# Splitting the operands of the last two FFN groups: which engine does which step, when the second weights are split, and where the pieces are kept

## The chip, the cores and the metric

The kernel runs on one core of one Trainium2 chip. The metric is device time in microseconds (us), the median of several executions. One more execution of each kernel is taken with the hardware profiler; its own time and its span are given beside the median. The core has five engines with a queue each: TensorE (PE, matrix products; its weight loads are shown as PEld), VectorE (DVE), ScalarE (ACT), GpSimd (POOL) and SyncE (SP, which issues most DMAs). Each engine takes its instructions in the order in which the program was built; an instruction that waits holds up everything behind it on its engine.

## The reference

Eight sequences of 576 tokens with eight heads of 64 go through an attention whose scores are cut off below the row's maximum less tau; the result, 4608 tokens of 512 numbers, goes through a feed-forward layer (FFN) with an ELU. Everything is float32.

```python
scores = scale * np.matmul(q, k.transpose(0, 1, 3, 2))
thresh = np.max(scores, axis=-1, keepdims=True) - tau
scores = np.where(scores >= thresh, scores, -1000000000.0)
attn = np.exp(scores - np.max(scores, axis=-1, keepdims=True))
attn = attn / (np.sum(attn, axis=-1, keepdims=True) + 1e-09)
x = np.matmul(attn, v)                       # bridged to (4608, 512)
h = x @ w_in                                 # w_in  512 x 2048
g = np.where(h > 0.0, h, np.exp(np.minimum(h, 0.0)) - 1.0)
out = g @ w_out                              # w_out 2048 x 512
```

## The kernel before, in words

**Groups.** The FFN works on nine groups of 512 tokens: eight hold the first 512 tokens of each sequence, and the ninth collects the 64 last tokens of all eight (`xtail`). Group 0 is done plainly, groups 1 to 6 by one level of Strassen's scheme in fp32 (lines 1675 and 1815), mixed with the attention of later sequences. For Strassen some blocks of the weights in SBUF have been replaced by differences (`change_in`, `change_out`); `restore_in` (L2055) and `restore_out` (L2059) add them back. The last Strassen group also needs sums of blocks of its hidden values, `sums` (L1762), which go through a queue of small jobs, `extra`, of which one is taken now and then (`run_extra`). While attention is still running (`attending`), these sums are GpSimd's. The adds at L1824 to L1835 take Strassen products out of the PSUM banks; the next product in the bank waits for them.

**The last two groups**, g7 and g8 (B - 1 and B), are done in split precision. An operand X is cut into a rounded part a = X(1 - 2^-13) held as fp32r, on ScalarE (`cut`, L1997; for weights L2021), and a rest b = X - a (`rest`, L2001; for weights L2026), and a cross piece is made from both (`cross`, L2005; for weights L2032). Three fp32r matmuls on these pieces stand in for one fp32 matmul. For weights the rest is also scaled by 2^12 (`weights_scaled`, L2029). The split of a token part costs an ACT step, a two-operand step on VectorE or GpSimd (an argument says which), and a VectorE step. The split of a weight tile costs an ACT step, a two-operand step on GpSimd, an ACT step, and a VectorE step.

**First product.** For each of 16 rows f of 128 hidden units and each of the two groups, `first_round` (L2182) runs eight matmuls into one of eight PSUM banks, ACT scales the bank (L2186), and `cross_round` (L2195) adds four more. Then come the exponential (ACT, L2206), minus one (GpSimd, L2209) and the ELU (VectorE, L2212). The five first rows of g7 go ahead, so that the parts of g8 have time to be made. **Second product.** `second` (L2261) runs three matmuls for each row and each of four token blocks; all of g7, then all of g8, with the first three and the last three rows taken block by block (`EDGE`). The cross weights of g8 are made afresh (L2252). At the end of a group each block's two banks are put together by ACT (L2276) and VectorE (L2278) and stored.

**Order.** This tail is written with a clock of its own: `at(t, f)` puts an instruction on an agenda at an estimated time, and `on_pe` records everything due before each piece of TensorE's work. The times fix the order in every queue, and nothing else; the hardware's waits do the rest. `UNIT` and `ONE` are the estimated times of twelve matmuls and of one.

**Places.** The pieces live in 24 slots on the right of SBUF (`r0` to `r23`) and 34 on the left (`l0` to `l33`), taken from the front of `free` and given back at its end. Names in the profile are those of the slots. The rounded part of eight second-weight rows goes into the upper half of the first weights, dead by then (`w_in_hi`); raw hidden values of the later rows go into the lower half (`w_in_lo`) and into token tiles (`xt`).

Of the kernel before, what the change touches and what calls it, by code (L numbers as in the profile page):

```python
# [368 lines left out]
def kernel(  # L369
# [10 lines left out]
    nc = tc.nc  # L380
# [61 lines left out]
    HF = DF // 2  # L442
    w_in_sb = [const.tile([P, KJ, HF], FP32, name=x) for x in ("w_in_lo", "w_in_hi")]

    def w_in_at(j, f, n):
        return w_in_sb[f // HF][:, j, f % HF : f % HF + n]

    w_out_sb = const.tile([P, NFT, DM], FP32, name="w_out_sb")
# [13 lines left out]
    pieces += [(moe_w_out, w_out_sb[:, f, n : n + WN], f, n) for f in range(NFT) for n in range(0, DM, WN)]  # L462
# [683 lines left out]
    def ffn2_plain(c, i, part):  # L1146
        def run(k):
# [3 lines left out]
            nc.tensor.matmul(cur[c, i][:, :DM], hidden(c, ft % NU, 1)[:, 0, ft // NU, i], w_out_sb[:, ft],  # L1151
# [101 lines left out]
    def make_out(r):  # L1253
        rooms = []

        def one(k, p):
# [3 lines left out]
            b12, b11 = w_out_sb[:, u : u + 2, HM:], w_out_sb[:, u : u + 2, :HM]  # L1260
            b21, b22 = w_out_sb[:, NU + u : NU + u + 2, :HM], w_out_sb[:, NU + u : NU + u + 2, HM:]
# [10 lines left out]
    def change_out(u):  # L1272
        b12, b11 = w_out_sb[:, u : u + 2, HM:], w_out_sb[:, u : u + 2, :HM]
        extra.append((1.3, "out", lambda: nc.gpsimd.tensor_tensor(b12, b12, b11, ALU.subtract)))
# [337 lines left out]
    with tc.manual_schedule():  # L1612
# [172 lines left out]
        def second_round(g, r):  # L1785
            banks_ = []

            def chunk(c):
# [5 lines left out]
                def quarter(m, k):  # L1794
# [15 lines left out]
                    for v in range(2 * k, 2 * k + 2):  # L1810
# [3 lines left out]
                               w_out_sb[:, right[1] * NU + u, right[2] * HM : (right[2] + 1) * HM])  # L1814
# [153 lines left out]
        free, parts, split_stack = deque(), {}, ExitStack()  # L1968
# [5 lines left out]
        def slot(dt):  # L1974
            pool, name = home = free.popleft()
            return pool.tile([P, DM], dt, name=name), home

        def drop(key, *which):
            for x in which or range(len(parts[key])):
                if parts[key][x] is not None:  # L1980
                    if parts[key][x][1]:
                        free.append(parts[key][x][1])
                    parts[key][x] = None
# [15 lines left out]
        def rest(key, src, engine, cols=slice(0, DM), fresh=True):  # L1999
            b = take(key, F32R) if fresh else parts[key][1][0]  # L2000
            engine.tensor_tensor(b[:, cols], src()[:, cols], parts[key][0][0].bitcast(FP32)[:, cols], ALU.subtract)  # L2001
# [6 lines left out]
        def split_tokens(t, key, src, engine):  # L2008
            at(t, lambda: cut(key, src))
            at(t + 0.8, lambda: rest(key, src, engine))  # L2010
            at(t + (0.8 if engine is nc.gpsimd else 1.5), lambda: cross(key, src))

        def weights_cut(key, src):
            if key[0] == "out" and EDGE <= key[1] < EDGE + NU:
# [312 lines left out]
```

## Time and profile before

| | us |
|---|---|
| median of 3 runs (lowest to highest) | 1275.36 (1274.95 to 1275.61) |
| profiled execution, its own time | 1273.53 |
| its span in the profile | 1271.7 |
| end of the last wide attention step's products (L1815 follows) | 1048.2 |
| first split matmul (L2182) | 1082.3 |
| first matmul of the second product (L2261) | 1173.5 |
| last matmul ends | 1267.0 |

Busy time in four stretches of the tail, in us: Strassen's end, the first product, the second product of g7 with its edges, the second product of g8.

| stretch | PE | DVE | ACT | POOL |
|---|---|---|---|---|
| 1050 to 1077 | 23.77 | 15.42 | 5.88 | 16.48 |
| 1100 to 1165 | 65.00 | 25.18 | 38.07 | 35.09 |
| 1165 to 1215 | 46.82 | 49.93 | 31.55 | 30.36 |
| 1215 to 1272 | 52.04 | 37.33 | 12.09 | 15.47 |

A timeline line gives start, duration, engine, line of the program, operation, tiles written and read, shapes and count; in brackets the engine's idle time before it and what ended that. Matmuls overlap, so the pace is read from starts, not from durations. On VectorE, ScalarE and GpSimd an instruction's record also holds time in which it stood but could not go on.

### The profile page before, as it was taken

What the parts mean: (1) busy time and instruction counts of PE and PEld (TensorE: products, weight loads), DVE (VectorE), ACT (ScalarE), POOL (GpSimd) and SP (SyncE); (2) the same over time, 40 slices, a digit from 0 to 9 for tenths busy, and PEclk for the clock granted to TensorE, in tenths of its full rate; (3) what the DMA queues carried; (4) which work ended last, traced back from release to release, by engine and by line L of the source; (5) the groups of instructions that cost most, each with busy time, mean ns of one, the idle gap of its engine ahead of it and who ended that gap; (6) DMA issues with size and microseconds to landing.
All of it is one profiled execution on the core that took longest, in us unless ns stands there. A gap on an engine that the chain in (4) does not pass through costs nothing.

```text
span 1271.7 us, 21210 instructions
## 1 busy us (share of the span) xinstructions
PE 1246.8 (98%) x6598; PEld 957.3 (75%) x6598; DVE 1035.4 (81%) x2146; ACT 651.2 (51%) x1363; POOL 804.6 (63%) x1114
## 2 busy tenths in 40 slices
PE   8999999999999999999999999999999998999998
PEld 5675576467778787878887787878787886788876
DVE  7888777788898979898889888997989885635994
ACT  7899776664443525262535344443525261556630
POOL 4778665677585748585676657674768475466650
PEclk9999999999999999999999999999999999999999
DMA  7466688998889998999889898989899864000001
GB/s 142 147 174 186 170 244 233 258 269 208 229 228 258 239 252 231 250 247 229 236 238 276 217 234 215 252 241 233 231 265 249 228 198 149 3 1 1 1 34 34
DMA packets 325553, 245.75 MB, mean 193 GB/s; under 512 B 209216, under 2 KB 289984, under 8 KB 325440
## 3 DMA queue, kind: packets, MB, share of 16 engines
q1 hardware_dynamic: 323264, 243.65, 71.6%
q8 instruction: 52, 0.85, 0.3%
q10 hardware_dynamic: 2176, 0.75, 0.2%
q14 instruction: 61, 0.50, 0.1%
HBM read 154.53 MB, written 89.78 MB: 192 GB/s over the span
## 4 chain that ended last, share of the span: by engine, by line
PE 87%; DVE 5%; issue 2%; DMA 2%; ACT 2%; POOL 1%; SPq 1%; ACTq 0%; DVEq 0%; POOLq 0%
PE f L1815 22%; PE f L1675 22%; PE sc L974 8%; PE sc L1047 7%; PE f L2182 4%; PE f L1099 4%; PE f L2261 4%; PE sc L670 3%; PE f L1151 3%; PE pv L927 2%; PE f L2195 2%; PE rt L789 1%; PE sc L1039 1%; PE sc L1034 1%; DMA there<-x 1%
## 5 line engine op out<-in xcount | busy, mean ns | idle before, releaser
L981 DVE TENSOR_REDUCE mx<-sc 128x1 f32<-128x576 f32 x207 | 148.3, 750 | 29.2 <-PE sc L974 25.2
L723 POOL TENSOR_SCALAR w<-w,rs 128x576 f32<-128x576 f32 x144 | 116.3, 816 | 70.4 <-DVE rs L786 69.7
L1001 ACT ACTIVATE w<-sc,mx 128x576 f32<-128x576 f32 x113 | 81.5, 739 | 115.1 <-DVE mx L981 98.1
L865 DVE STREAM_TRANSPOSE x<-w 128x512 f32<-128x512 f32 (+1 forms) x153 | 108.9, 744 | 14.0 <-POOL w L723 11.3
L993 POOL TENSOR_SCALAR th<-mx,ntau 128x2 f32<-128x2 f32 (+1 forms) x114 | 34.1, 299 | 132.8 <-DVE mx L981 132.8
L974 PE MATMUL sc<-kT,qT 64*128 64x448 f32 (+4 forms) x736 | 102.8, 416 | 0.0
L974 PEld LDWEIGHTS sc<-kT,qT 64*128 64x128 f32 x736 | 81.0, 186 | 24.3 <-issue 16.2
L1008 DVE SCALAR_TENSOR_TENSOR w<-sc,th,w 128x576 f32<-128x576 f32 x113 | 88.2, 810 | 9.5 <-ACT w L1001 9.2
L1815 PE MATMUL f<-t,s 128*128 128x256 f32 x384 | 91.7, 380 | 3.2 <-POOL s L1762 3.1
L1675 PE MATMUL f<-xt,sw 128*128 128x256 f32 x384 | 93.6, 386 | 0.7 <-ACT g L1737 0.5
L1815 PE MATMUL f<-w_out_sb,g 128*128 128x256 f32 x384 | 92.0, 382 | 0.0
L1815 PE MATMUL f<-w_out_sb,s 128*128 128x256 f32 x384 | 91.9, 382 | 0.0
L723 POOL TENSOR_SCALAR e<-e,rs 128x576 f32<-128x576 f32 x91 | 67.3, 744 | 35.2 <-DVE rs L786 33.8
L1815 PEld LDWEIGHTS f<-t,s 128*128 128x128 f32 x384 | 72.5, 190 | 14.9 <-POOL s L1762 5.2
L1675 PEld LDWEIGHTS f<-xt,sw 128*128 128x128 f32 x384 | 69.3, 189 | 17.3 <-issue 5.0
L1815 PEld LDWEIGHTS f<-w_out_sb,g 128*128 128x128 f32 x384 | 72.0, 190 | 12.5 <-issue 3.2
L1815 PEld LDWEIGHTS f<-w_out_sb,s 128*128 128x128 f32 x384 | 71.9, 190 | 12.1 <-issue 2.5
L1762 POOL TENSOR_TENSOR s<-g 128x256 f32<-128x256 f32 x96 | 75.9, 795 | 7.3 <-DVE g L1725 6.8
L1001 ACT ACTIVATE e<-sc,mx 128x576 f32<-128x576 f32 x91 | 66.5, 744 | 24.6 <-DVE mx L981 23.2
L1008 DVE SCALAR_TENSOR_TENSOR e<-sc,th,e 128x576 f32<-128x576 f32 x91 | 71.2, 810 | 7.6 <-ACT e L1001 7.6
L865 DVE STREAM_TRANSPOSE x<-e 128x640 f32<-128x640 f32 x92 | 66.0, 755 | 1.0
L727 DVE TENSOR_REDUCE mx<-sc 128x1 f32<-128x576 f32 x81 | 59.3, 747 | 5.5 <-PE sc L670 5.1
(323 smaller groups left out, 3283.7 us busy)
## 6 DMA issues: line engine op xcount, KB each, us to landing
there<-x SPq DMA_DIRECT2D x444, 144.0 KB, 3.6
wTb<-there SPq DMA_DIRECT2D x58, 576.0 KB, 6.3
wTa<-there SPq DMA_DIRECT2D x53, 576.0 KB, 5.1
sw<-win_sums SPq DMA_DIRECT2D x46, 384.0 KB, 4.8
t<-wout_sums SPq DMA_DIRECT2D x33, 512.0 KB, 6.3
qm<-in_q_dram SPq DMA_DIRECT2D x124, 72.0 KB, 4.9
wst<-in_moe_w_in_dram SPq DMA_DIRECT2D x16, 512.0 KB, 4.2
vm<-in_v_dram SPq DMA_DIRECT2D x64, 128.0 KB, 3.6
```

What stands on the lines that cost most here:

```text
L723: nc.gpsimd.tensor_scalar(wv, wv, st["rs"][:, h : h + 1], 1.0, ALU.mult, ALU.mult)
L727: nc.vector.tensor_reduce(st["mx"][:, h : h + 1], st[h][:, :, :HALF], axis=AX.XY, op=ALU.max, negate=True)
L865: nc.vector.transpose(x[:, :, c0 : c0 + nc_], src.rearrange("p (c g n) -> p g c n", c=nc_, n=T))
L974: on_banks(nc.tensor.matmul(o, qT[r, i * P : (i + 1) * P], kT[r, k0 : k0 + n], start=True, stop=True, skip_group_check=True), o)
L981: on_banks(nc.vector.tensor_reduce(st["mx"][:, h : h + 1], st["sc", h], axis=AX.XY if i == NC else AX.X, op=ALU.max, negate=True), st["sc" ...
L1001: on_banks(nc.scalar.activation(st["e", h], st["sc", h], AF.Exp, bias=st["mx"][:, h : h + 1]), st["sc", h])
L1008: on_banks(nc.vector.scalar_tensor_tensor(st["e", h], st["sc", h], st["th"][:, h : h + 1], st["e", h], ALU.is_ge, ALU.mult, accum_out=st[" ...
L1047: on_banks(nc.tensor.matmul(o, vm[:, h, c], parts[part][:, g0:g1, h * (NC + 1) + c], start=False, stop=(c == NC - 1), skip_group_check=Tru ...
L1099: nc.tensor.matmul(loc["ph"][:, k], w_in_at(j, ft * P, P), xts[g][:, j, hf * CT : (hf + 1) * CT], start=(j == 0), stop=(j == KJ - 1))
L1675: nc.tensor.matmul(loc["banks"][place], left[:, j], right[:, j], start=(begins and j == 0), stop=(j == 1), skip_group_check=True)
L1762: engine.tensor_tensor(o, x, y, op)
L1815: nc.tensor.matmul(place(m), lhs, rhs, start=(begins and v == 0), stop=(v == RU - 1), skip_group_check=True)
```

## The change

- Every two-operand step of the splits is VectorE's: the rests of tokens and of weights, and `restore_out`. The weights' rest becomes scaled on GpSimd (a one-operand step) instead of ACT, and the weights' cross piece is a plain subtraction on VectorE, made for second weights once for each group (`cross, g, f`) and no longer at their split.
- Eleven of the sixteen second-weight rows are split beside the first product, from 22 us after its start, one every 3.9 us; `restore_out` begins at 16 us, every 3.6 us.
- The weights lie in four tiles each (`w_in0` to `w_in3`, `w_out0` to `w_out3`) instead of two halves and one tile. When the last row of a quarter is split, `give` hands the quarter on as four slots for pieces of one type, which are taken ahead of the others. The token tiles are handed on likewise. The tiles kept for raw hidden values go.
- Before the first product three weight tiles are split instead of two, all eight lower restores are done there, and of g8 only one token part. Splitting begins one us earlier on the agenda.
- When splitting begins, `attending` is set to False, which gives the Strassen sums but the third to VectorE; in the last pair's step the jobs of `extra` are put on the agenda 1.9 us apart.
- Four rows of g7 go ahead, not five; the estimated times are raised.
- For the last token block the matmuls of the last three rows run first for the first bank (and the rest pieces), then for the cross pieces, and ACT's scaling is recorded between them.

```diff
-    w_in_sb = [const.tile([P, KJ, HF], FP32, name=x) for x in ("w_in_lo", "w_in_hi")]
+    w_in_sb = [const.tile([P, KJ, QF], FP32, name=f"w_in{x}") for x in range(4)]
+    w_out_sb = [const.tile([P, NFT // 4, DM], FP32, name=f"w_out{x}") for x in range(4)]
...
+        def give(pool, name, dt):
+            t = pool.tile([P, KJ, DM], dt, name=name)
+            kept_for[dt].extend(t[:, x] for x in range(KJ))
+
-        def slot(dt):
+        def slot(dt, wide=True):
+            if kept_for[dt]:
+                t = kept_for[dt].popleft()
+                return t, lambda: kept_for[dt].append(t)
             pool, name = home = free.popleft()
...
-        def rest(key, src, engine, cols=slice(0, DM), fresh=True):
+        def rest(key, src, cols=slice(0, DM), fresh=True):
             b = take(key, F32R) if fresh else parts[key][1][0]
-            engine.tensor_tensor(b[:, cols], src()[:, cols], parts[key][0][0].bitcast(FP32)[:, cols], ALU.subtract)
+            nc.vector.tensor_tensor(b[:, cols], src()[:, cols], parts[key][0][0].bitcast(FP32)[:, cols], ALU.subtract)
...
-            engine.tensor_tensor(like(d[0], src()), src(), like(parts[key][0][0].bitcast(FP32), src()), ALU.subtract)
+            d = take(("d", key), FP32)
+            nc.vector.tensor_tensor(like(d, src()), src(), like(parts[key][0][0].bitcast(FP32), src()), ALU.subtract)
 
         def weights_scaled(key):
-            nc.scalar.activation(take(key, F32R), parts["d", key][0][0], AF.Copy, scale=1.0 / EPS)
+            nc.gpsimd.tensor_scalar(take(key, F32R), parts["d", key][0][0], 1.0 / EPS, None, ALU.mult)
 
         def weights_cross(key):
-            nc.vector.scalar_tensor_tensor(take(key, F32R), parts["d", key][0][0], 1.0 / EPS,
-                                           parts[key][0][0].bitcast(FP32), ALU.mult, ALU.subtract)
-            drop(("d", key))
+            c, d = (parts[key][x][0].bitcast(FP32) for x in range(2))
+            nc.vector.tensor_tensor(take(key, F32R), d, c, ALU.subtract)
...
-        def split_weights(t, key, src, engine):
+        def split_weights(t, key, src, then=None):
             at(t, lambda: weights_cut(key, src))
-            at(t + 0.7, lambda: weights_rest(key, src, engine))
-            end = t + (2.3 if engine is nc.gpsimd else 1.6)
-            at(end, lambda: weights_scaled(key))
-            at(end + 0.1, lambda: weights_cross(key))
+            at(t + 0.7, lambda: (weights_rest(key, src), then and then()))
+            at(t + 1.4, lambda: (weights_scaled(key), drop(("d", key))))
+            if key[0] == "in":
+                at(t + 2.1, lambda: weights_cross(key))
...
-            nc.gpsimd.tensor_tensor(b12, b12, b11, ALU.add)
+            nc.vector.tensor_tensor(b12, b12, b11, ALU.add)
...
+        EARLY_IN = 3
 
         def split_begin():
             t = now[0]
+            attending[0] = False
...
+            for f in range(EARLY_IN):
+                at(t + 0.2 + 3.2 * f, lambda f=f: restore_in(f))
+                split_weights(t + 0.6 + 3.2 * f, ("in", f), w_in_of(f))
             for j in range(KJ - 1):
-                split_tokens(t + 0.2 + 2.2 * j, ("x", B - 1, j), x_of(B - 1, j), nc.vector)
-            for f in range(2):
-                at(t + 6.6 + 3.0 * f, lambda f=f: restore_in(f))
-                split_weights(t + 7.2 + 3.0 * f, ("in", f), w_in_of(f), nc.gpsimd)
-            for j in range(2):
-                split_tokens(t + 13.0 + 2.4 * j, ("x", B, j), x_of(B, j), nc.vector)
+                split_tokens(t + 2.2 + 3.2 * j, ("x", B - 1, j), x_of(B - 1, j))
+            split_tokens(t + 12.0, ("x", B, 0), x_of(B, 0))
+            for f in range(NU, NFT):
+                at(t + 11.0 + 1.2 * (f - NU), lambda f=f: restore_in(f))
...
-                at(t + 13.0, split_begin)
+                at(t + 12.0, split_begin)
+                for x in range(8):
+                    at(t + 1.0 + 1.9 * x, lambda: run_extra(max(0.9, extra[0][0])) if extra else None)
...
-        UNIT, ONE = 2.58, 0.215
+        UNIT, ONE, LEAD, AHEAD = 2.73, 0.2272, 8.0, 4
...
+        for j, t in ((1, 0.9), (2, 4.6), (last, 7.4)):
+            split_tokens(begin + t, ("x", g8, j), x_of(g8, j),
+                         (lambda: [give(xpool, "xt", FP32) for _ in range(2)]) if j == last else None)
...
+        for f in range(EARLY_IN, NFT):
+            t = max(begin + 0.4 + 3.4 * (f - EARLY_IN), start_of[g7, f] - LEAD)
+            if f < NU:
+                at(t - 0.5, lambda f=f: restore_in(f))
+            split_weights(t, ("in", f), w_in_of(f), lambda f=f: in_done(f))
         for u in range(NU):
-            at(begin + 30.0 + 5.0 * u, lambda u=u: restore_out(u))
+            at(begin + 16.0 + 3.6 * u, lambda u=u: restore_out(u))
...
+        OUT_EARLY = 11
         for f in range(NFT):
...
+            split_weights(begin + 22.0 + 3.9 * f if f < OUT_EARLY else start_f(middle, f) - 9.0, ("out", f), w_out_of(f),
+                          lambda f=f: out_done(f))
+            for g, t0 in ((g7, middle), (g8, end)):
+                t = start_f(t0, f) - (9.5 if f < EDGE else 6.0) + 2.9 * f * (f < EDGE)
+                split_tokens(t, ("h", g, f), g_of(g, f), lambda g=g, f=f: drop(("g", g, f)))
+                at(t + 2.2, lambda g=g, f=f: nc.vector.tensor_tensor(
+                    take(("cross", g, f), F32R), parts["out", f][1][0].bitcast(FP32), parts["out", f][0][0].bitcast(FP32),
+                    ALU.subtract))
...
+        def edge(g, fs, i):
+            if (g, i) == (g8, 3) and fs[-1] == NFT - 1:
+                return [(lambda f=f, xs=xs: second(g, f, i, xs), len(xs) * ONE) for xs in ((0, 1), (2,)) for f in fs]
+            return [(lambda f=f: second(g, f, i), 3 * ONE) for f in fs]
```

146 lines of the change are left out of this document (59 added, 87 removed).

## The prediction

> **What bounds the kernel now.** I read the page's busy shares first, then the chain of work that ended last, then the waits of the last 240 us, then the timelines of TensorE (PE), VectorE (DVE) and GpSimd (POOL) there, because the order in which the changed program is built agrees with the old one on every engine up to about 1050 us. Only the last two of nine FFN groups differ, and the sums that end the group before them.
>
> ```profile
> PE 1246.8 (98%) x6598; PEld 957.3 (75%) x6598; DVE 1035.4 (81%) x2146; ACT 651.2 (51%) x1363; POOL 804.6 (63%) x1114
> ```
>
> TensorE is the bound, so a gain can only come from time in which it does not stream. The waits name who keeps it (total, times, longest):
>
> ```profile
> PE f L2261 <- DVE r L2032: 3.2, 2, 2.5
> PE f L1815 <- POOL s L1762: 3.1, 2, 2.9
> PE f L2182 <- ACT l L2029: 3.1, 3, 1.1
> ```
>
> TensorE's timeline shows where; the bracket is the idle time and what ended it:
>
> ```profile
> 1071.55 2.26 PE L1815 MATMUL f<-t,s 128*128 128x256 f32 x8 [2.88 <-POOL s L1762]
> ...
> 1087.54 1.88 PE L2182 MATMUL f<-r,l 128*128 128x512 f32 x7 [1.01 <-ACT l L2029]
> ...
> 1091.63 1.88 PE L2182 MATMUL f<-r,l 128*128 128x512 f32 x7 [1.08 <-ACT l L2029]
> ...
> 1095.63 1.88 PE L2182 MATMUL f<-r,l 128*128 128x512 f32 x7 [0.98 <-ACT l L2029]
> ```
> ```profile
> 1176.19 0.50 PE L2261 MATMUL f<-r,r 128*128 128x512 f32 x1 [0.70 <-DVE r L2032]
> ...
> 1188.26 0.39 PE L2261 MATMUL f<-w_in_hi,l 128*128 128x512 f32 x1
> ...
> 1193.81 0.39 PE L2261 MATMUL f<-w_in_hi,l 128*128 128x512 f32 x1
> ...
> 1213.46 0.78 PE L2261 MATMUL f<-r,l 128*128 128x512 f32 x1 [2.47 <-DVE r L2032]
> 1214.04 0.63 PE L2261 MATMUL f<-r,r 128*128 128x512 f32 x1
> ...
> 1216.99 0.40 PE L2261 MATMUL f<-l,l 128*128 128x512 f32 x1
> ...
> 1222.43 0.39 PE L2261 MATMUL f<-r,l 128*128 128x512 f32 x1
> ```
>
> Two paces are to be read off. From 1216.99 to 1222.43 there are 24 matmuls, 0.2267 us each. From 1188.26 to 1193.81 there are also 24, 0.2313 each: one of every three reads its moving operand from the reused tile w_in_hi. That is 0.0046 x 3 = 0.0138 us per such matmul. Why the late operands are late stands in the timelines of VectorE and GpSimd:
>
> ```profile
> 1126.45 1.14 DVE L2032 SCALAR_TENSOR_TENSOR l<-l,l 128x512 fp32r<-128x512 f32 x1
> 1131.17 0.68 DVE L2032 SCALAR_TENSOR_TENSOR l<-l,l 128x512 fp32r<-128x512 f32 x1
> ...
> 1205.21 1.78 DVE L2032 SCALAR_TENSOR_TENSOR l<-l,l 128x512 fp32r<-128x512 f32 x1
> 1206.91 1.78 DVE L2001 TENSOR_TENSOR l<-xt,l 128x512 fp32r<-128x512 f32 x1
> ```
> ```profile
> 1126.43 0.62 POOL L2209 TENSOR_SCALAR l<-l 128x512 f32<-128x512 f32 x1 [0.62 <-ACT l L2206]
> ...
> 1204.80 3.34 POOL L2026 TENSOR_TENSOR l<-w_out_sb,r 128x512 f32<-128x512 f32 x2 [1.26 <-ACT r L2021]
> ```
>
> A two-operand step of VectorE takes 0.68 us alone (0.60 from start to start). Next to a two-operand step of GpSimd it takes 1.78, a delay of 1.10, and next to a one-operand one 1.14, a delay of 0.46.
>
> **What TensorE loses from 1050 us on**, at the paces above:
> - (a) Strassen tail, 1050.07 to 1077.19: 13 groups of eight matmuls at 1.727 us (first starts 1050.07, 1051.80) are 22.5 of 27.1 us: 4.6 lost, 3.0 at the wait for the sum L1762.
> - (b) First product, 1082.34 to 1098.26: 52 matmuls are 11.8 of 15.9 us: 4.1 lost.
> - (c) At 1176.19 the matmul starts 0.9 late.
> - (d) End of the first group's second product: 2.6 late at 1213.46, and then 8 matmuls in 3.53 us instead of 1.81, 1.7 more. Together 4.3.
> - (e) 192 matmuls at the slower pace: 192 x 0.0046 = 0.9.
> - (f) From the last matmul's end (1267.03) to the span's end 1271.7.
>
> **The change, part by part.**
>
> (a) The Strassen sums but the third of each four go from GpSimd to VectorE and are recorded 1.9 us apart; the two-operand L2026 (1.27 us, and it waits 1.96 and 1.62 in front of the sums) leaves GpSimd. So the 2.88 wait has no cause left. But in the built order VectorE now holds 43 instructions between the start of the splits and the first split matmul, 28 before: three weight tiles prepared instead of two, eight more restores (nine with the third tile's), four sums. At 0.34 us per 256-wide and 0.60 per 512-wide one that is 29 x 0.34 + 14 x 0.60 = 18.3 us instead of 16 x 0.34 + 12 x 0.60 = 12.6, in some 28 us. The adds that free a bank (L1833, L1835), for which TensorE waits, stand in this queue behind splits: four places where two or three steps (0.9 to 1.6 us) lie in front. I count 1.2 + 0.9 + 1.3 + 0.7 = 4.1 lost for 4.6: -0.5. Ends: -4.6 (no loss left) and +2.4 (the 5.7 us added, less the 3.3 that VectorE idled before its steps at 1055.45, 1057.18 and 1061.21: 1.30, 1.30, 0.74).
>
> (b) Three weight tiles are split before TensorE begins, not two, and four rows of the first group, not five, come ahead of the second group's. The fourth tile is needed after 28 matmuls, 6.3 us in; recorded at 0.4 us, its chain of restore 0.34, cut 0.62, rest 0.68, scaled 0.62 is 2.3 us plus a queue of one or two steps. Covered with 2 to 3 us to spare. The last token part is recorded at 7.4 and used after 10.4, with 0.62 + 0.68 of chain: 1.7 to spare. So -4.1. Ends: -4.1 and -3.0 (one gap of 1.1 stays, the nearest row).
>
> (c) The cross step takes two operands on VectorE and waits for no GpSimd subtraction: -0.9; ends -0.9 and 0.
>
> (d) Eleven of sixteen second-weight splits are moved beside the first product. There each pair of steps of TensorE (24 matmuls, 5.44 us) now has on VectorE 0.6 + 0.6 + 2 x 0.6 of its own and 0.94 x 5.44 / 3.9 = 1.3 of moved work, 3.7 us, beside (1 + 2 + 1.4) x 0.46 = 2.0 us of GpSimd's. Even if every GpSimd instruction held VectorE up, 5.7 is only 0.3 over, and the 8 us lead covers eight pairs of that (2.3). In the second product VectorE has 3 x 0.60 = 1.8 us per 2.72 us, 2.4 + 0.46 = 2.86 for the last five rows. At the end three rows are needed at once: in the built order 17 VectorE steps (10.2 us) and four held steps (1.8) stand from the thirteenth row's weight split to the first cross matmul of the edge, where TensorE has some 46 matmuls, 10.4 us: 12.0 - 10.4 = 1.6 us late instead of 2.6. Is there a slow stretch behind it? The 2.47 wait had one; waits of 0.70 to 1.08 had none (1.88 for seven at 1087.54 as at 1095.63). 1.6 is nearer to 1.08: I take none. So 4.3 - 1.6 = 2.7 gained; ends -4.3 and 0. [...]
>
> (e) In the built order 136 of the 384 matmuls of the second product read their moving operand from reused weight quarters, 64 before; 160 more read only the stationary one there, which no row prices. 136 x 0.0138 - 0.9 = +1.0. Ends: -0.9 (none slow) and +4.1 (all 360 that touch one, the first product's 64 included).
>
> (f) The last token block's scaling is moved ahead of its last matmuls, so the two half adds (0.76 together from 1267.35) start when TensorE ends, at 1267.03 and a semaphore: -0.25; ends -0.7 (the scaling pair's 0.66) and 0. The stores behind are as before.
>
> Scaled copies leave ACT (51% busy) for GpSimd: nothing on the path, the 0.46 above is their price. DMA order is the same. Sum: -0.5 - 4.1 - 0.9 - 2.7 + 1.0 - 0.25 = -7.5 us. The profiled execution took 1273.53 (span 1271.7), 1.8 below the median of the three runs, 1275.36. So 1266.1 for such an execution, and **1267.9** for a median.
>
> **The rivals.**
> 1. *Better still*: the Strassen tail flows and reused quarters cost nothing (a -3, e -0.9): 1263.5. For it: only one engine's queue has to be short. Against: 43 steps in it. 0.15.
> 2. *The Strassen tail waits for VectorE* (a +2.4): 1270.8. For it: bank-freeing adds behind splits. Against: 18.3 of 28 us. 0.12.
> 3. *GpSimd's one-operand steps hold VectorE up so far in the first product that the lead is used up*: 0.3 us per pair, eight pairs, +2.3: 1270.2, with one more such step per pair (0.46 x 8) 1273.9. For it: 1.14 against 0.68. Against: VectorE idled 40 of 65 us there (25.2 busy from 1100 to 1165). 0.10. [...]
> 4. *Slower: VectorE becomes the bound of the second product.* Its three steps per row and group have 2.72 us. Held up each time, as 1165.67 (1.17) was, 3 x 1.1 = 3.3: 0.6 x 32 = 19 us, 1287. It decides from 0.32 us a row, steps of 1.01 (10 us lost against 7.5 gained). Against: GpSimd has only five instructions left in that stage. 0.06.
> 5. *The waits only move*: the edge keeps its 4.3, the first product two gaps of 1.1, and quarters stand at their dear end: -0.5 - 1.9 - 0.9 + 4.1 - 0.25 = +0.5, 1275.9. For it: 360 matmuls touch a quarter. Against: fp32 matmuls of earlier stages keep one pace whichever tile they read (1.727 for eight throughout). 0.07.
>
> **How the numbers follow.** 0.50 is left for the forecast (1265 to 1271 with its own ends of a and e partly drawn). The measurement tells 0.2% (2.55 us) from no change: faster is below 1272.8, slower above 1277.9. Rivals 1 to 3 and the forecast are faster, 0.87, less a little for 3's dear end: 0.85; same 0.08; slower 0.07. The range runs from rival 1, 1263.0, to between rivals 3's two ends, 1272.3.
>
> **What would show it.** Right: no TensorE wait above 0.3 us in the first 20 us after the first split matmul; the wait at the group edge 1 to 2 us, released by VectorE; VectorE steps of 1.78 us gone, 1.14 left; 24 matmuls in 5.55 us over most of the second product. Wrong: TensorE waits in the middle of either product, or half pace behind the edge.

## The result and the profile after

The changed kernel took 1285.22 us in the median (1284.42 to 1286.68, four executions) against 1275.15 (1273.09 to 1275.61) of the kernel before: a ratio of 1.0083, 95% interval 1.0066 to 1.0101. It is 10 us slower where 7.5 us less had been forecast. The profiled execution took 1286.68 us, its span is 1284.9.

The page's busy shares of the changed kernel (the same line as was shown of the kernel before):

```profile
PE 1253.4 (98%) x6598; PEld 959.7 (75%) x6598; DVE 1039.1 (81%) x2199; ACT 635.6 (49%) x1331; POOL 784.4 (61%) x1093
```

TensorE still has 98%, and GpSimd is even less busy than before (784.4 us for 804.6). The shares say nothing of what went wrong. A table by stage does. The three stretches below run from the first Strassen matmul after 1045 us to the first split matmul, from there to the first matmul of the second product, and to the last matmul's end; the columns are the length and each engine's busy time with its number of instructions, then TensorE's granted clock and the DMA share. First the kernel before, then the changed one:

```profile
core 0: us, PE busy (x) PEld busy (x) DVE busy (x) ACT busy (x) POOL busy (x), PEclk, DMA share, GB/s
1048.24:1082.34 34.10, 30.87 (x154) 23.54 (x153) 17.82 (x30) 7.35 (x16) 17.78 (x19) 1.00 0.40 141
1082.34:1173.51 91.17, 88.10 (x387) 71.97 (x385) 46.42 (x70) 56.05 (x104) 50.08 (x56) 1.00 0.01 1
1173.51:1267.03 93.52, 90.34 (x385) 72.89 (x383) 78.06 (x92) 35.22 (x64) 39.27 (x23) 0.98 0.05 18
```
```profile
core 0: us, PE busy (x) PEld busy (x) DVE busy (x) ACT busy (x) POOL busy (x), PEclk, DMA share, GB/s
1050.07:1086.47 36.40, 31.13 (x155) 23.55 (x153) 21.70 (x45) 6.18 (x14) 15.33 (x16) 1.00 0.38 132
1086.47:1189.16 102.69, 92.63 (x386) 74.00 (x385) 59.02 (x97) 50.55 (x94) 62.26 (x53) 0.97 0.01 1
1189.16:1280.12 90.96, 89.75 (x385) 71.83 (x383) 65.90 (x103) 25.89 (x46) 9.66 (x8) 1.00 0.06 18
```

The second product is 2.56 us shorter, close to the forecast (c, d and e together: -2.6). The first product is 11.52 us longer where 4.1 less was expected, and the Strassen tail 2.3 longer. (The tail also begins 1.83 us later. Nearly all of that is no effect of the change: in this execution TensorE's granted clock was 0.50 from 259.33 to 262.74 us, which costs 1.7 us of work, and in the profiled execution of the kernel before it was 1.00 there. The changed kernel with a single instruction's form edited, below, began the tail at 1048.23.)

TensorE's timeline in the first product of the changed kernel; the bracket is the idle time and what ended it:

```profile
1126.30 3.35 PE L2187 MATMUL f<-r,l 128*128 128x512 f32 x7 [2.93 <-POOL l L2031]
1140.80 1.89 PE L2187 MATMUL f<-r,r 128*128 128x512 f32 x7 [1.66 <-POOL r L2031]
1148.73 0.50 PE L2187 MATMUL f<-r,l 128*128 128x512 f32 x1 [2.19 <-POOL l L2031]
1156.81 1.90 PE L2187 MATMUL f<-r,w_out 128*128 128x512 f32 x7 [0.71 <-POOL w_out L2031]
1165.13 1.90 PE L2187 MATMUL f<-r,l 128*128 128x512 f32 x7 [2.57 <-POOL l L2031]
```

Five waits, 10.06 us, all released by L2031, the scaled copy that the change gave to GpSimd, and all far behind the place where the old kernel's three waits of 1.0 had been. Those are gone, as (b) said. The instruction itself, in an answer on its line (minimum/median/maximum in ns):

```profile
L2031 POOL TENSOR_SCALAR l<-xt x9: 1489/1492/1868, 1102.4 to 1215.8; 128x512 fp32r<-128x512 f32 x9
```

These nine, and the other 23 steps of this line, take 1.49 us or more. The prediction had put 0.62; the one GpSimd step on a single tensor that it shows, L2209 (now L2214) on the same shape, takes that.

### The profile page after: what moved, and what is told of

The parts are those of the page before. It is cut to its first block, busy times and chain, and to the rows that moved or that the text cites. A ratio compares the mean times of both kernels' runs of the same rounds, so it can differ in the third digit from the quotient of the medians.

```text
span 1284.9 us, 21199 instructions
## 1 busy us (share of the span) xinstructions
PE 1253.4 (98%) x6598; PEld 959.7 (75%) x6598; DVE 1039.1 (81%) x2199; ACT 635.6 (49%) x1331; POOL 784.4 (61%) x1093
## 5 line engine op out<-in xcount | busy, mean ns | idle before, releaser
L984 DVE TENSOR_REDUCE mx<-sc 128x1 f32<-128x576 f32 x207 | 148.3, 750 | 29.8 <-PE sc L977 25.8
L1818 PE MATMUL f<-w_out,s 128*128 128x256 f32 x384 | 92.1, 383 | 2.1 <-DVE ot L1836 1.6
L1678 PE MATMUL f<-xt,w_in 128*128 128x256 f32 x384 | 91.8, 382 | 0.5 <-ACT w L1692 0.5
L1818 PE MATMUL f<-w_out,g 128*128 128x256 f32 x384 | 92.0, 382 | 0.0
L1678 PE MATMUL f<-x,w_in 128*128 128x256 f32 x384 | 90.8, 379 | 0.0
L1818 PEld LDWEIGHTS f<-w_out,s 128*128 128x128 f32 x384 | 71.8, 190 | 14.8 <-issue 2.5
L1818 PEld LDWEIGHTS f<-w_out,g 128*128 128x128 f32 x384 | 72.0, 190 | 12.5 <-issue 3.2
L1678 PEld LDWEIGHTS f<-xt,w_in 128*128 128x128 f32 x384 | 72.0, 190 | 12.5 <-ACT w L1692 2.7
L1678 PEld LDWEIGHTS f<-x,w_in 128*128 128x128 f32 x384 | 72.9, 190 | 10.1 <-ACT s L1692 0.3
```

The lines of the kernel that those rows point to most:

```text
L984: on_banks(nc.vector.tensor_reduce(st["mx"][:, h : h + 1], st["sc", h], axis=AX.XY if i == NC else AX.X, op=ALU.max, negate=True), st["sc" ...
L1678: nc.tensor.matmul(loc["banks"][place], left[:, j], right[:, j], start=(begins and j == 0), stop=(j == 1), skip_group_check=True)
L1818: nc.tensor.matmul(place(m), lhs, rhs, start=(begins and v == 0), stop=(v == RU - 1), skip_group_check=True)
```

## The experiments

The theory after this reading, A: the scaled copy's *form* is slow. It is a one-tensor step with one operation (times 4096), while the row that priced it has two (times 1, minus 1). Rivals: B, the slowness comes of writing fp32r; C, the steps stand in the wrong order in the queues, and their length matters little; D, the reuse of slots makes ScalarE's exp wait for a tile that GpSimd has yet to read. Four kernels tell these apart.

**A second operation.**

```diff
-            nc.gpsimd.tensor_scalar(take(key, F32R), parts["d", key][0][0], 1.0 / EPS, None, ALU.mult)
+            nc.gpsimd.tensor_scalar(take(key, F32R), parts["d", key][0][0], 1.0 / EPS, 1.0, ALU.mult, ALU.mult)
```

> The scaled step on GpSimd (L2031) is given a second operation, times 1.0, and is else as it was: same engine, same operands, same fp32r output, same place in the queue. Theory A (the form with one operation is what costs 1.49 us): each of the 27 to 32 steps takes about 0.62 as the two-operation step L2214 does, the five TensorE waits of the first product (2.93, 1.66, 2.19, 0.71, 2.57) and the two half-pace stretches go, the first product shrinks from 102.7 us to 87 to 90 and the time falls from 1285 by 12 to 15 us, to 1270 to 1273. Rival B (writing fp32r through a one-tensor step of GpSimd is slow): the steps stay at 1.49 and the time at 1285 within 1 us. Rival C (the order of the queues, not the length of the step): the steps fall to 0.62, but at least 5 us of waits stay, 1278 or more.

Measured: 1267.05 us, ratio to the kernel before 0.9933 (0.9918 to 0.9947). The line's answer, the stages, and the whole list that the profile gives of what TensorE waited for from 1050 us on (total, times, longest):

```profile
L2031 POOL TENSOR_SCALAR l<-xt x9: 622/732/1001, 1097.9 to 1196.5; 128x512 fp32r<-128x512 f32 x9
```
```profile
1048.23:1081.99 33.76, 31.12 (x154) 23.55 (x152) 21.68 (x45) 6.20 (x14) 12.68 (x16) 1.00 0.42 143
1081.99:1169.80 87.81, 87.81 (x386) 72.21 (x385) 59.83 (x97) 50.83 (x94) 41.44 (x53) 1.00 0.01 1
1169.80:1260.75 90.95, 89.79 (x385) 71.78 (x383) 65.90 (x103) 25.96 (x46) 5.85 (x8) 1.00 0.06 18
```
```profile
PE f L1818 <- DVE ot L1836: 1.7, 2, 1.0
PE f L2264 <- DVE l L2253: 1.2, 1, 1.2
PE f L1818 <- DVE s L1765: 0.5, 1, 0.5
PE f L1818 <- DVE ot L1838: 0.4, 1, 0.4
```

One operand more in one line, 0.62 us at the least and 0.73 in the median of these nine instead of 1.49, and 18.2 us of the time are gone: A holds. In the first product TensorE is busy for all of 87.81 us. B falls (the output is still fp32r) and C falls. Between the two profiled executions 14.9 us come from the first product (102.69 to 87.81), 2.6 from the tail (36.40 to 33.76), where three of the slow steps stand, and 1.8 from the earlier begin of the tail, which is not the edit's (the stretch at half clock above). The gain is above the 12 to 15 us expected, which had not counted the tail.

**The scaled copy back on ScalarE.**

```diff
-            nc.gpsimd.tensor_scalar(take(key, F32R), parts["d", key][0][0], 1.0 / EPS, None, ALU.mult)
+            nc.scalar.activation(take(key, F32R), parts["d", key][0][0], AF.Copy, scale=1.0 / EPS)
```

> The scaled step goes back to ScalarE (activation Copy with scale, as in the kernel before); everything else as changed. Theory A and rival B (GpSimd's step is the cause, whichever part of its form): 0.62 us a step on an engine with 50% idle, waits of the first product gone, 1270 to 1274. Rival C or D (order of the queues, or ScalarE's exp waiting for a slot that a split still reads): the scaled copies and the cuts are then in ScalarE's queue together with the exp, so a late exp holds them as well: 5 us of waits or more stay, 1278 to 1290.

Measured: 1264.91 us, ratio 0.9914 (0.9900 to 0.9929), again below the range expected. The same result from the other side, and a little better than the GpSimd step with a second operation: the tail is 33.17 us (33.76), and the wait at the group edge, 1.15 with that step, is gone, so the second product takes 89.75 (90.95). That VectorE is no longer held up by GpSimd's copies would explain it; it was not tried by itself.

**No second-weight splits beside the first product**, with the slow step left in.

```diff
-        OUT_EARLY = 11
+        OUT_EARLY = 0
```

> No second-weight tile is split beside the first product: all sixteen at the pace of the second product, nine us ahead of use. Theory A (steps of 1.49 us, each with a subtraction of 0.62 to 1.1 behind it): GpSimd has one slow step per pair of TensorE's rows instead of two, so the first product's waits fall from 10 us to under 2 and its half pace goes; the second product then has 3 to 4 steps on VectorE per 2.72 us and GpSimd 1.49, and loses 3 to 8 us. 1275 to 1282. Rival D (slots): the input splits alone keep the coupling of exp to split, the first product keeps 5 us or more of waits, 1283 to 1292.

Measured: 1275.94 us, 1.0003 (0.9994 to 1.0013). The first product shrinks from 102.69 to 91.70 and none of its waits is released by L2031 any more; the second grows from 90.96 to 93.57. With one slow step per pair of TensorE's rows instead of two, GpSimd keeps up. The expectation missed in one thing: a wait of 3.27 us for ScalarE's L2191 stands at the end of the first product, with half clock behind it (the granted clock is 0.91 over 1160 to 1180 us), where under 2 us and no half clock were expected.

**Two slots for the intermediate tile alone.**

```diff
-            d = take(("d", key), FP32)
+            d = take(("d", key), "d")
...
-                         (lambda: [give(xpool, "xt", FP32) for _ in range(2)]) if j == last else None)
+                         (lambda: [give(xpool, "xt", FP32) for _ in range(2)] + [kept_for["d"].append(kept_for[FP32].popleft()) for _ in range(2)]) if j == last else None)
```

> The intermediate of a weight split (the tile d, written by L2028 and read by L2031) gets two slots of its own, so that no exp on ScalarE (L2211) takes a slot that GpSimd still has to read; the slow step itself stays. Rival D (the coupling by slots makes ScalarE late, and with it the cuts of the next splits): ScalarE's waits for L2031 (3.4 to 4.9 us) go and the first product's TensorE waits fall from 10 us to under 4: 1274 to 1279. Theory A (GpSimd's queue is late by itself): TensorE's waits stay within 3 us of 10, and the time within 4 us of 1285; VectorE may wait for GpSimd in its place.

Measured: 1284.74 us, 1.0069 (1.0054 to 1.0084). ScalarE no longer waits for L2031 anywhere (once it waits 6.4 us for VectorE's L2028 instead), so the edit did its part, but the first product takes 102.86 us with waits of 2.92, 1.63, 0.89, 2.26 and 2.57, 10.3 together. D falls.

**How can a step of 1.49 us do this?** In the changed kernel's first product GpSimd is busy 62.26 of 102.69 us. It idles 40. The timelines of VectorE and GpSimd up to the first wait show why that doesn't help:

```profile
1121.10 0.69 DVE L2217 SCALAR_TENSOR_TENSOR xt<-xt,f 128x512 f32<-128x512 f32 x1 [1.58 <-POOL xt L2214]
1121.71 0.42 DVE L2057 TENSOR_TENSOR w_out<-w_out 128x256 f32<-128x256 f32 x1
1122.04 0.68 DVE L2028 TENSOR_TENSOR xt<-w_out,l 128x512 f32<-128x512 f32 x1
1122.64 0.68 DVE L2028 TENSOR_TENSOR w_in<-w_in,l 128x512 f32<-128x512 f32 x1
1126.28 0.69 DVE L2035 TENSOR_TENSOR l<-l,l 128x512 fp32r<-128x512 f32 x1 [2.95 <-POOL l L2031]
```
```profile
1118.87 1.49 POOL L2031 TENSOR_SCALAR l<-xt 128x512 fp32r<-128x512 f32 x1
1120.44 0.62 POOL L2214 TENSOR_SCALAR xt<-xt 128x512 f32<-128x512 f32 x1
1122.81 1.87 POOL L2031 TENSOR_SCALAR l<-xt 128x512 fp32r<-128x512 f32 x1 [1.74 <-DVE xt L2028]
1124.76 1.49 POOL L2031 TENSOR_SCALAR l<-w_in 128x512 fp32r<-128x512 f32 x1
```

Read it as a ring. GpSimd's subtraction (L2214, 1120.44) stands behind a slow copy. VectorE's L2217 waits 1.58 us for it. Both next rests (L2028) stand behind L2217. GpSimd waits 1.74 us for the first of them, then copies the second-weight tile (1.87) before the first-weight tile that TensorE needs (1.49, ends 1126.25). TensorE starts at 1126.30, after 2.93 us. The two engines take turns waiting for each other, so both show idle time while the pair is the bound. The same order of events stands before the second, fourth and fifth wait, where L2217 waits 2.38, 2.31 and 1.58 us for a subtraction behind a slow copy; before the third, L2028 waits 0.89 us for the slot that the copy is still reading. If that is the cause, opening the ring must help even with the slow copy left as it is:

```diff
             def minus():
-                nc.gpsimd.tensor_scalar(loc["h"], loc["h"], 1.0, -1.0, ALU.mult, ALU.add)
+                nc.vector.tensor_scalar(loc["h"], loc["h"], 1.0, -1.0, ALU.mult, ALU.add)
```

> The changed kernel with its slow scaled step left on GpSimd; the subtraction of 1 behind the exp (L2214), 32 times, goes from GpSimd to VectorE. It asks how a step of 1.49 us makes TensorE wait while GpSimd idles 24 of 80 us. Theory R (a ring: the subtraction stands behind the slow step in GpSimd's queue, VectorE's L2217 waits for the subtraction, the next split's L2028 stands behind L2217 in VectorE's queue, and GpSimd's next slow step waits for that): with the subtraction out of GpSimd's queue the ring is open, GpSimd has 24 slow steps, 36 us in 87, and the first product's waits fall from 10 us to under 2: 1270 to 1274. Rival L (the slow step by its own length and its place in one queue makes the operand late): waits of 5 us or more for L2031 stay, 1279 or more.

Measured: 1273.85 us, 0.9986 (0.9975 to 0.9996); the first product takes 90.31 us. What is left of the five waits, in TensorE's timeline:

```profile
1142.63 0.50 PE L2187 MATMUL f<-r,l 128*128 128x512 f32 x1 [1.13 <-POOL l L2031]
1154.41 1.89 PE L2187 MATMUL f<-r,l 128*128 128x512 f32 x7 [0.42 <-POOL l L2031]
```

The slow steps are all there (none of L2031's 32 takes less than 1488 ns), and 8.5 of 10 us of waits are gone. Theory R, the ring, holds, and rival L falls: the length of the step matters because it is an arc of a ring. The edit also takes 32 steps off GpSimd, but GpSimd had 40 us to spare, and none of its subtractions between 1107 and 1166 us had kept it idle.

**The forms by themselves.** Behind the last matmul of the changed kernel, three rounds of these steps and their like, on 128x512 unless it says 256 (one execution, 1317.20 us):

```diff
+            nc.gpsimd.tensor_scalar(mbr, mbs, 1.0 / EPS, None, ALU.mult)
+            nc.gpsimd.tensor_scalar(mbd, mbs, 1.0 / EPS, None, ALU.mult)
+            nc.gpsimd.tensor_scalar(mbr, mbs, 1.0 / EPS, 1.0, ALU.mult, ALU.mult)
...
+            nc.gpsimd.tensor_scalar(mbd, mbs, 1.0, None, ALU.add)
...
+            nc.gpsimd.tensor_scalar(mbd[:, :256], mbs[:, :256], 1.0 / EPS, None, ALU.mult)
+            nc.gpsimd.tensor_scalar(mbd[:, :256], mbs[:, :256], 1.0 / EPS, 1.0, ALU.mult, ALU.mult)
...
+            nc.vector.tensor_scalar(mbr, mbs, 1.0 / EPS, None, ALU.mult)
+            nc.vector.tensor_scalar(mbr, mbs, 1.0 / EPS, 1.0, ALU.mult, ALU.mult)
```

> The changed kernel with thirty one-tile steps on GpSimd and six on VectorE put behind its last matmul, three of each form, on 128x512 elements, VectorE idle while GpSimd runs: it only measures the forms. Theory A (one operation instead of two is slow on GpSimd): times 4096 alone takes about 1.49 us into fp32r and into plain fp32 alike, and so do plus 1.0 alone and a product with a per-partition scalar; with a second operation 0.62 into either type; 128x256 elements take about half of each. Rival: only a product by an immediate, or only the fp32r output without a second operation, is slow: then plus 1.0 alone, or fp32 output, takes 0.62. VectorE: both forms alike, 0.3 to 0.7. The span is longer by their sum, some 35 us.

The costliest groups from 1280 us on, behind the last matmul (busy us, mean ns): L2308 and L2309 are the one-operation product into fp32r and fp32, L2310 the two-operation one into fp32r, L2312 the one-operation sum, L2315 and L2316 the 256-wide pair, L2319 and L2320 VectorE's pair:

```profile
L2312 POOL TENSOR_SCALAR w_in<-w_in 128x512 f32<-128x512 f32 x3 | 4.5, 1495 | 0.2
L2309 POOL TENSOR_SCALAR w_in<-w_in 128x512 f32<-128x512 f32 x3 | 4.5, 1489 | 0.2
L2308 POOL TENSOR_SCALAR w_out<-w_in 128x512 fp32r<-128x512 f32 x2 | 3.0, 1490 | 0.2
L2315 POOL TENSOR_SCALAR w_in<-w_in 128x256 f32<-128x256 f32 x3 | 2.5, 849 | 0.2
L2310 POOL TENSOR_SCALAR w_out<-w_in 128x512 fp32r<-128x512 f32 x3 | 1.9, 620 | 0.2
L2316 POOL TENSOR_SCALAR w_in<-w_in 128x256 f32<-128x256 f32 x3 | 1.2, 406 | 0.2
```
```profile
L2319 DVE TENSOR_SCALAR w_out<-w_in 128x512 fp32r<-128x512 f32 x3 | 1.3, 427 | 31.2 <-POOL w_out L2317 31.1
L2320 DVE TENSOR_SCALAR w_out<-w_in 128x512 fp32r<-128x512 f32 x3 | 1.3, 427 | 0.1
```

A product alone or a sum alone costs 1.49, into either type (1.57 with a scalar for each partition); a product followed by a product or a sum costs 0.62. From 256 to 512 elements that is (1.490 - 0.849) / 256 = 2.50 ns an element against (0.620 - 0.406) / 256 = 0.84, three times as much, over a fixed part of 0.2 in both. On VectorE the two forms take the same 0.427.

It is not the number of operations alone, though. Two steps of the kernel before on tiles of the same name and shape, both with two operations, are far apart: L1109 (times 1, then minus 1) and L1121 (the smaller of the value and 1, then minus 1):

```profile
L1109 POOL TENSOR_SCALAR g<-g x13: 614/627/1062, 61.3 to 208.4; 128x512 f32<-128x512 f32 x13
L1121 POOL TENSOR_SCALAR g<-g x3: 1917/1937/1948, 166.5 to 193.1; 128x512 f32<-128x512 f32 x3
```

So what is shown is a price for each of these operations and pairs; why the pairs that begin with a product are cheap is open.

**The prediction's other steps**, each with the short step in:

```diff
-        OUT_EARLY = 11
+        OUT_EARLY = 0
```

> Scaled step with a second operation, and none of the second weights split beside the first product (all sixteen nine us ahead of use). The prediction's step (d) (the splits beside the first product cost nothing there, and spare VectorE in the second product): the first product stays at 87.8 us, within 0.5; the second, 90.95 with eleven splits moved, has a fourth VectorE step in every row of the first group, 2.4 us and what GpSimd holds up, 2.9 to 3.3 per 2.72 us, and grows by 1.5 to 4 us, with waits at its group edge: 1268.5 to 1271. Rival (the place of the splits is worth nothing once the step is short): 1267 within 0.8.

Measured: 1271.04 us, 0.9971 (0.9960 to 0.9983), 4 us above the same kernel with eleven early splits. The second product takes 93.60 us (90.95), but most of that is the clock: waits of 0.32 and 1.47 us at the group edge (1.15 with eleven early splits) are followed by a stretch at half pace (starts 0.43 us apart from 1208.10 to 1209.81, 0.23 from 1210.54 on), 1.7 us. The waits alone grew by 0.64, so what the early splits spare VectorE there is small by itself. The first product took 89.15, 1.3 more and not within 0.5, with one wait of 1.57 for ScalarE's L2191 at its end.

```diff
             t = now[0]
-            attending[0] = False
             attention.close()
...
                 at(t + 12.0, split_begin)
-                for x in range(8):
-                    at(t + 1.0 + 1.9 * x, lambda: run_extra(max(0.9, extra[0][0])) if extra else None)
```

> Scaled step with a second operation; the last Strassen sums as in the kernel before, on GpSimd and without their new spacing; three weight tiles still split and eight restores still made before the first product. The prediction's step (a) (the sums' move and spacing takes the 2.88 us wait away, the longer VectorE queue gives most of it back): with only the second half left, the stretch from the first Strassen group of the round to the first split matmul grows from 33.8 to 35 to 37 us: 1268.5 to 1271. Rival (with the two-operand subtraction gone from GpSimd the sums are in time there too, and VectorE is spared four steps): 33.8 or less, 1265 to 1267.

Measured: 1268.97 us, 0.9954 (0.9939 to 0.9968). The tail takes 35.41 us (33.76 with the sums moved) and waits for the sums again:

```profile
1060.59 1.13 PE L1818 MATMUL f<-t,s 128*128 128x256 f32 x4 [1.67 <-POOL s L1765]
1064.33 1.13 PE L1818 MATMUL f<-w_out,s 128*128 128x256 f32 x4 [1.75 <-POOL s L1765]
1066.32 2.26 PE L1818 MATMUL f<-t,s 128*128 128x256 f32 x8 [0.86 <-POOL s L1765]
```

So the move and spacing of the sums is worth 1.65 us of the tail, even with GpSimd's two-operand subtraction gone. Then two attempts to go further, both on the kernel with the copy on ScalarE. Four restores later:

```diff
-            for f in range(NU, NFT):
+            for f in range(NU, NU + 4):
                 at(t + 11.0 + 1.2 * (f - NU), lambda f=f: restore_in(f))
...
-            if f < NU:
-                at(t - 0.5, lambda f=f: restore_in(f))
+            if f < NU or f >= NU + 4:
+                at(t - 0.5 if f < NU else begin + 2.0 + 1.7 * (f - NU - 4), lambda f=f: restore_in(f))
```

> Scaled copy on ScalarE, and four of the eight restores of the first weights (L2053) moved from in front of the first product into it, where VectorE idles a third of the time. Theory (a) (TensorE waits in the Strassen tail, 2.6 us in four waits with the copy on ScalarE, because the adds that free its banks stand behind restores and splits in VectorE's queue): 4 x 0.34 = 1.4 us less in front of them, 0.7 to 1.4 us faster than 1264.9, so 1263.5 to 1264.2. Rival (the adds wait for something else, ScalarE's copies of the banks or the splits themselves): 1264.9 within 0.5.

Measured: 1264.06 us, 0.9921 (0.9906 to 0.9935), which is not apart from 0.9914. (The time by itself lies in the theory's range, but the kernel before was also 1.1 us faster beside this run, 1274.25 for 1275.37.) The tail is 32.85 us (33.17): of its four waits 0.40, 0.60 and 1.04 stay and only the last goes from 0.55 to 0.21. For three of the four waits these restores were not what stood in front.

The weight quarters 32 bytes further on:

```diff
     QF = DF // 4
+    eight = const.tile([P, 1], I32, name="eight")
...
-    eight = const.tile([P, 1], I32, name="eight")
     nc.gpsimd.memset(eight, 8)
```

> Scaled copy on ScalarE, and the one-element tile 'eight' allocated in front of the weight quarters instead of behind them, so that every quarter starts 32 bytes further on: the quarters then stand, as the other split tiles do, 32 bytes past a multiple of 64; nothing else moves in the last stage. It tests step (e). Theory (the start address of a reused quarter sets the slower pace, 0.2333 us a matmul against 0.2267): the pace of the second product goes back to about 0.227, the two products shrink from 87.8 and 89.75 us by about 0.5 and 2.0, and 1264.9 becomes 1262 to 1263. Rival (something else of the quarters, their place or who wrote them, or the second product's own pattern): the pace stays at 0.233 and the time at 1264.9 within 0.7.

Measured: 1264.92 us, 0.9922 (0.9907 to 0.9937): no gain that the time shows. The products take 87.71 and 89.03 us (87.79 and 89.75). The second got 0.7 faster, not 2, so the start address is at most a third of what was to be explained.

> All that helped so far: scaled copy on ScalarE, four restores moved into the first product, the quarters shifted by 32 bytes. If the shift sets the pace, about 0.5 us below the run with the shift alone, 1261.5 to 1262.5; if it does not, 1264 to 1265.

Both together: 1263.52 us, 0.9913 (0.9899 to 0.9927), against 0.9914 with the copy on ScalarE alone. That is between the two ranges expected and decides for neither. The best kernels of this study are therefore the changed one with the copy on ScalarE, with or without these two edits: 0.9% faster than the kernel before and 1.6 to 1.7% faster than the changed one (1264.91 and 1263.52 against 1285.22).

## Why the prediction was wrong

**The term that failed** is the price of the scaled copy on GpSimd. It stands in (b) as "scaled 0.62", in (d) only as 0.46 us by which it holds VectorE up, and behind (f) as "Scaled copies leave ACT (51% busy) for GpSimd: nothing on the path, the 0.46 above is their price". The row of that engine and shape that the prediction shows, L2209, multiplies and then adds; the new instruction only multiplies, and takes 1.49. No wide GpSimd step with one operation is in the trace of before. So the price should have been bounded from both sides, and the dear end was in plain sight: GpSimd's two-operand steps L2026 at 1.26 to 1.74, and L1121, on one tensor and the same shape, at 1.92 or more. That end was never written down, and the range stayed without it. In (b) the wrong price did no harm, since its 2 to 3 us to spare covered it; in (d) it did.

**The cover that failed with it** is (d)'s "Even if every GpSimd instruction held VectorE up, 5.7 is only 0.3 over, and the 8 us lead covers eight pairs of that". This adds up busy time on one engine. With 24 steps 0.87 dearer, busy time alone would still have found room on GpSimd (62 of 103 us). What it leaves out is the round trip: copy, subtraction, L2217, rest, next copy, in two in-order queues that wait for each other. The run with the subtraction on VectorE shows that it is this ring which turned a slow step into 10 us of waits, and of the 15.6 us that the first product lost against an unbroken 384 x 0.2267 = 87.05, these 10 are the largest part; two stretches at half clock behind them (1.7 each, below) and the slower pace of (e) are most of the rest.

With the second operation added, and nothing else, the time was 1267.05 for a forecast of 1267.9. That it came so close is in part luck: the medians are 8.3 us apart and the profiled executions 6.2, for 7.5 forecast. The other terms can be checked one by one on that kernel (differences to the profile of before):

- (a) -0.5: right. 33.76 for 34.10 is -0.34. With the slow step it was +2.3, the size of rival 2, for another reason: VectorE itself waited 1.40, 1.02 and 1.27 us there for L2031, and the adds behind it came late.
- (b) -4.1: right, in both. 52 matmuls from 1086.47 on took 11.9 us in the changed kernel, 15.9 before.
- (c) -0.9: right. No wait stands at the start of the second product.
- (d) -2.7 at the group edge: right. The wait is 1.21 in the changed kernel and 1.15 with the short step (1.6 forecast), at full clock, released by VectorE. Taking 1.3 as lost, it gained 3.0. The prediction took "none" for the half clock from the length of the wait; in these traces the half clock went with the busy part of a fixed stretch (last section). In the changed kernel that is 2.20 of 3.41 us from 1225.31, with a granted clock of 1.00 in the next, so here it came out the same.
- (e) +1.0: too small, +2.3. The second product's 383 steps from start to start, without the edge, take (90.55 - 1.3) / 383 = 0.2330 us, 2.4 over the pace of 0.2267 for 384, where it was 0.9 before; and the first product is 0.76 over 384 x 0.2267 = 87.05. Weights read as the stationary operand from a reused quarter cost too, which "no row prices": 63 such matmuls of the first product start 0.2331 us apart, the others 0.2274. The dear end of +4.1 had allowed for them. What makes those reads slower is open: the shift by 32 bytes did not settle it.
- (f) -0.25: +0.1 here, and open. The last adds start 0.49 us after the last matmul's start instead of 0.70, but the span ends 4.7 behind their start instead of 4.35. From the last matmul's end to the span's end it is 4.77 us in this kernel and 4.70 before; six of the other edited kernels, with the same ending, have 4.46 or 4.47, as forecast. What decides between the two is not shown.

The sum of these is -0.3 - 4.1 - 0.9 - 3.0 + 2.3 + 0.1 = -5.9, and the span is 6.2 shorter (1265.5 for 1271.7). The good match of the second product, -2.56 for -2.6, is in part two errors that cancel: more gained in (d), more lost in (e).

Of the rivals, 3 was nearest, since it named GpSimd's steps and a lead used up; but it had them hold VectorE up at 0.46 each and capped the loss at 6 us. (The two delays that it went by, 0.46 and 1.10, are each shorter than the GpSimd step beside them, 0.62 and 1.67; the rows show no more of their size than that.) Rival 4, the slower one, had VectorE in the second product, and that stage is 2.56 us shorter. The sign that had been named for a wrong prediction, waits in the middle of either product, is what appeared.

## What to carry to other kernels

Price a moved step by a row with the same engine, the same form and the same operations; where there is none, the dear end belongs in the range, and a second operation that changes nothing (times 1.0) or another engine belongs among the alternatives. Where two in-order engines feed each other, a stage can be bounded by the time around their ring and not by the busier of them, as here, with 10 us of waits for a GpSimd that was busy 62.26 of 102.69 us: write the ring down (who waits for whom, and what is queued between) before calling a step covered. An engine that is 61% busy, as GpSimd was there, can have no room left if it idles while it waits for the other half of the ring.

## What the hardware showed that was not expected

**One operation on GpSimd can be dearer than two**: on 128x512 elements 1.49 us for a product or a sum alone, 0.62 for a product and then a product or a sum, 1.92 or more for the smaller of two and then a sum, as above. Between 256 and 512 elements the product alone took 2.50 ns an element and the pair of products 0.84; VectorE's whole step of 0.427 us is 0.83 an element.

**In these traces half clock went with the busy part of fixed stretches of 3.41 us, not with the length of a wait.** The prediction argued from lengths: half pace behind 2.47, none behind 1.08. In the changed kernel the wait of 2.19 brought half clock and that of 2.57 did not. The stretches before and behind the waits of 2.93, 2.19 and 2.57 us, all cut on one grid of 3.41 us laid through the first half-clock stretch (first column behind the length is TensorE's busy time, the column behind the five engines the granted clock):

```profile
1122.91:1126.32 3.41, 0.48 (x4) 0.06 (x2) 0.46 (x2) 0.00 (x0) 3.26 (x2) 1.00 0.00 0
1126.32:1129.73 3.41, 3.41 (x8) 2.74 (x9) 2.88 (x5) 0.59 (x2) 2.25 (x3) 0.50 0.03 5
1146.80:1150.21 3.41, 1.48 (x6) 1.23 (x7) 1.22 (x3) 2.60 (x5) 2.62 (x2) 1.00 0.00 0
1150.21:1153.62 3.41, 3.41 (x9) 2.63 (x8) 1.10 (x3) 2.12 (x4) 2.11 (x2) 0.50 0.01 2
1160.46:1163.87 3.41, 2.10 (x10) 1.40 (x8) 1.70 (x3) 0.33 (x1) 2.05 (x2) 1.00 0.00 0
1163.87:1167.28 3.41, 2.15 (x9) 1.78 (x10) 1.65 (x3) 2.51 (x6) 2.92 (x3) 1.00 0.02 5
```

The second half-clock stretch begins 23.89 us after the first, seven times 3.413, and the first 866.99 us after the one at 259.33 in the same execution, 254 times 3.4133. The wait of 2.57 is cut in two by the grid at 1163.87, leaves 2.10 and 2.15 us busy in its two stretches, and costs no clock. In the kernel with two slots for the intermediate tile, a stretch with 1.52 us busy was followed by half clock and one with 1.68 was not:

```profile
1060.72:1064.13 3.41, 1.52 (x8) 1.02 (x7) 3.06 (x6) 1.15 (x2) 0.99 (x2) 1.00 0.00 0
1064.13:1067.54 3.41, 3.41 (x9) 2.18 (x8) 2.65 (x6) 0.98 (x2) 0.73 (x1) 0.50 0.24 82
1149.47:1152.88 3.41, 1.68 (x8) 1.03 (x6) 1.89 (x3) 3.05 (x7) 2.00 (x2) 1.00 0.00 0
1152.88:1156.29 3.41, 2.88 (x13) 2.37 (x14) 1.38 (x2) 0.58 (x1) 3.17 (x4) 1.00 0.00 0
```

So in these stretches the granted clock was 0.50 for the next 3.41 us where TensorE had been busy for 0.48, 1.48 and 1.52 us, and 1.00 where it had been busy for 1.68 or more; each half-clock stretch costs, by estimate, 3.41 / 2 = 1.7 us of work. The kernel before fits: 0.94 us busy from 1210.10 to 1213.51, with the wait of 2.47, then 0.50. Of all stretches at full clock between 1050 us and the last matmul in the traces of the kernel before and the changed one, on their grids, those with 1.48 us busy or less were followed by half clock and those with 1.93 or more were not. The limit is not sharp in these records: without early splits a stretch with about 1.7 us busy was followed by half pace (an estimate: by the starts of its matmuls the half pace lasts to about 1210.4, so it began near 1207.0, and the waits of 0.32 and 1.47 us fill about 1.7 of the 3.41 us before that). A wait of 1.9 can be enough (the one in the stretch from 1060.72 above), so were those of 0.32 and 1.47 together, and one of 2.6 can be harmless (2.57 above).
